# Expert weights prepared ahead of pass 0, their low halves on VectorE, and the order of loads and stores in a fused attention and mixture-of-experts kernel

## The chip, the cores and the metric

One core of a Trainium2 chip runs the whole program in one launch. The metric is device time in microseconds; shorter is better.

## The reference

Three stages, all in float32, one feeding the next:

```python
# 1. chunked attention: 4 batches x 8 heads x 768 positions x 64;
#    32 queries see 8 memory keys and the keys from 16 before to 8 behind their chunk
out[:, :, c0:c1] = softmax(scale * q_c @ k_full.T) @ v_full
x = out.transpose(0, 2, 1, 3).reshape(3072, 512)
# 2. gated feed-forward: w_gate, w_val (512 x 1536), w_out (1536 x 512)
x = (sigmoid(x @ w_gate) * (x @ w_val)) @ w_out
# 3. eight experts: w1 (8 x 512 x 1024), w2 (8 x 1024 x 512)
P = exp(x @ w_gate2 - max)
for _ in range(8):                 # Sinkhorn over experts and tokens
    P /= P.sum(1, keepdims=True) + 1e-9
    P /= P.sum(0, keepdims=True) + 1e-9
    P *= 3072 / 8
out = sum(P[:, e:e+1] * (relu(x @ w1[e]) @ w2[e]) for e in range(8))
```

## The kernel before

Every large product is made as three matmuls on operands split into a high half `h` (rounded by ScalarE) and a low half `l` (the source less `h`): `operand` (L116) is this pair of instructions, and the engine passed to it makes the low half. Many 2 x 2 block products go by a seven-product scheme, for which `combine` (L120) makes sums of blocks.

The tokens are eight chunks of 384. Chunks 0 and 1 go through feed-forward plainly, then three blocks `b` = 1 to 3 of two chunks each; beside each block runs the attention of later chunks. `hook` (L375) is called 60 times in a block (a tick), and `schedule` lays side work on tick numbers. `paced` (L426) puts what a step issues behind the last gated operand of feed-forward on the same engine. The order of instructions on each engine and of DMA issues on SP (all DMAs are issued there) comes from a planner that runs a timeline simulation while the program is built; `issue_after` adds an order between two instructions of one engine to what it may choose.

The expert stage runs three passes `s` of 1024 tokens over 8 experts with 2 halves `hf` of the hidden layer. A layer (one `e`, `hf`) has two units `fp`. `layer1` (L901) makes a unit's seven products `p` from W1; `layer2` (L970) makes eight token tiles `py` in pass 0, where W2 is used in full, and `layer2_turned` is for passes 1 and 2. The first three products of the next layer's first unit stand ahead of each `layer2`. In pass 0 the weights arrive raw. `ask` (L840) loads a unit's four raw tiles, two units before their use. `w1_operands` (L135) makes seven W1 tiles in the `ws` slots (nine) and stores them to `w1k`; `w2_get` (L862) makes W2's full tiles and stores them to `w2k`; `w2_sums` (L848), a layer2 later, makes the sums for passes 1 and 2 and stores them. For these units GpSimd makes all low halves. Passes 1 and 2 load `w1k` and `w2k` back (`w1_load`, L154; `w2_get`).

The first four units (`EN`, L49) are prepared during blocks 2 and 3 by `early_weights` (L611), ten steps a unit from tick 16 of block 2 on, two ticks apart. It reads each unit's raw W1 and raw W2 twice, 512 KB at a time, and pass 0 loads the results back. `first_x` (L664) makes the operands of three of the seven token sums of pass 0 at ticks 40 to 52 of block 3; `rest_of_x` (L670) makes the others at its end. Both call `x_part` (L176), which fetches a quarter of the tokens with 8 DMAs of 64 KB into one of the two `r` slots and uses it at once.

Sinkhorn (L751) runs beside layers 0 and 1 in 17 steps. `beat` (L797) is called at each of a unit's seven products and at each token tile of layer2; every third call makes a step. Its column sums go through TensorE (`pc`, L775), so TensorE waits there for VectorE's `cs` (L772). The last two steps store the gates for passes 1 and 2.

Of the kernel before, what the change touches and what calls it, by code (L numbers as in the profile page):

```python
# [47 lines left out]
XA, XB = 40, 4  # L48
EA, EB, EN = 16, 2, 4  # L49
XALL = True  # L50
XQ = ()
# [11 lines left out]
def moe_chain(ctx: ExitStack, tc: tile.TileContext, qkv, mask, mrow, mone, wa, wg, wb, out):  # L63
# [70 lines left out]

    def w1_operands(nm, r, pool, kept=None, ce=None, ge=None):  # L135
# [12 lines left out]
        operand(t[6][:, 0], t[6][:, 1], ge, a22)  # L148
        if kept is not None:
            for i in range(TH):  # L150
                nc.sync.dma_start(out=kept[i], in_=flat(t[i]).bitcast(F32))
        return w1_sets(t)

    def w1_load(nm, pool, kept):  # L154
        t = w1_tiles(nm, pool)
        for i in range(TH):
            nc.sync.dma_start(out=flat(t[i]).bitcast(F32), in_=kept[i])
        return w1_sets(t)

    early = {}  # L160
# [15 lines left out]
    def x_part(s, xop, kk, o, which=range(7)):  # L176
        xr = rw.tile([128, 2, 2, XW], F32, tag="r", name=f"xs{s}_{kk}_{o}_{which[0]}")
# [18 lines left out]
    with ExitStack() as c1:  # L196
# [414 lines left out]
        def early_weights(u):  # L611
            nm = "_".join(map(str, u))

# [5 lines left out]
            def split(q, src, n, kept):  # L619
                h = rw.tile([128, 1024], F32R, tag="r", name=f"eh{q}_{nm}")[:, 0:n]  # L620
                l = rw.tile([128, 1024], F32R, tag="st", name=f"el{q}_{nm}", bufs=SB_)[:, 0:n]
                operand(h, l, nc.vector, src)
# [4 lines left out]
            k1, k2 = w1k[u], w2k[u]  # L627
            ve = nc.vector
# [13 lines left out]
            operand(h[:, 0:512], h[:, 512:], ve, ld[:, 0])  # L642
            nc.sync.dma_start(out=k1[0], in_=h[:, 0:512].bitcast(F32))
            nc.sync.dma_start(out=k1[1], in_=h[:, 512:].bitcast(F32))
            h = rw.tile([128, 1024], F32R, tag="r", name=f"ea_{nm}")[:, 0:512]
            operand(h[:, 0:256], h[:, 256:], ve, q[3])
            nc.sync.dma_start(out=k1[6], in_=h.bitcast(F32))
            yield
# [10 lines left out]
            ld, _ = raw(1)  # L659
            yield  # L660
            split("d", flat(ld), 1024, [(k2[0], k2[1], 0, 1024)])
            yield

        def first_x():  # L664
            early["x"] = x_tiles(0, XE)
            for kk, o in parts:
                x_part(0, early["x"], kk, o, XE)
                yield

        def rest_of_x():  # L670
            rest = tuple(i for i in range(7) if i not in XE)
            early["x"].update(x_tiles(0, rest))
            for kk, o in parts:
                x_part(0, early["x"], kk, o, rest)
                yield

        pend = []
        for b in range(1, NCH // 2):
            if b == 2:
                schedule(clock[0] + EA, [paced(early_weights(u)) for u in early_units], EB * 10, range(0, 10 * EB, EB))  # L680
            if b < NCH // 2 - 1:
                schedule(clock[0] + CB[0], [attention(c, hp) for c in (2 * b + 2, 2 * b + 3) for hp in range(4)], CB[1], O3)
            else:
                c3.close()
                early["xe"] = ctx.enter_context(tc.tile_pool(name="xe", bufs=1, side="right", reuse_waits="tile"))
                schedule(clock[0] + XA, [paced(first_x())], XB, range(0, 4 * XB, XB))
# [48 lines left out]
            second(*pend.pop(0), halves=(1,))  # L735
            second(*pend.pop(0))
# [7 lines left out]
    with ExitStack() as c2:  # L744
# [52 lines left out]
        def beat():  # L797
            beats[0] += 1
            if beats[0] % 3 == 1:
# [4 lines left out]
        def x_operands(s):  # L804
            xop = x_tiles(s, range(7))
            for kk in range(2):
                for o in range(0, 512, XW):
                    x_part(s, xop, kk, o)
# [13 lines left out]
        def raw_pair(nm, src):  # L822
            rs = []
            for f, k in enumerate(("sh", "sl")):
                rs.append(s_tile(k, f"{nm}_{f}", F32))
                nc.sync.dma_start(out=rs[f], in_=src[:, f, :])
# [21 lines left out]
        def w2_sums():  # L848
# [9 lines left out]
            operand(th, tl, nc.gpsimd, v.rearrange("p i d -> p (i d)"))  # L858
# [3 lines left out]
        def w2_get(s, e, hf, fp):  # L862
# [11 lines left out]
            nc.sync.dma_start(out=dh.bitcast(F32), in_=kept[0])  # L874
            nc.sync.dma_start(out=dl.bitcast(F32), in_=kept[1])
# [25 lines left out]
        def layer1(s, e, hf, xop, gs, w2):  # L901
# [154 lines left out]
        xop = early["x"]  # L1056
        work = [(s, e, hf) for s in range(NSB) for e in range(E) for hf in range(2)]
# [89 lines left out]
```

## Time and profile before

| | us |
|---|---|
| median of 3 runs (2708.99 to 2713.59) | 2712.32 |
| the profiled execution | 2718.7 |
| its span, first to last instruction | 2716.9 |
| TensorE busy | 2646.9 |
| VectorE busy | 2058.4 |
| ScalarE busy | 1128.1 |
| GpSimd busy | 711.1 |

Feed-forward and attention fill the span to about 790 us, pass 0 of the experts goes on to about 1450 us, pass 1 to about 2070 us, pass 2 to the end. TensorE's busy time is high in every part, so the profile is read by stretches: where TensorE sits idle, what its granted clock is there, and what ended each wait. Busy shares of the other engines only matter where TensorE waits for one of them.

### The profile page before, as it was taken

How to read it: one execution, taken by the hardware profiler on the slowest of the kernel's cores; microseconds unless marked ns; L12 is line 12 of the kernel's file. 1: busy time of each engine (PE TensorE's matmuls, PEld its weight loads, DVE VectorE, ACT ScalarE, POOL GpSimd, SP SyncE). 2: the span in 40 equal slices, each digit the busy share in tenths (PEclk: the TensorE clock that was granted, in tenths of full speed). 3: DMA queues.
4: the chain of work that ended last, by engine and by line, in shares of the span. 5: the costliest groups of instructions: out<-in, count | busy, mean ns of one | idle time of the engine just before them, and what ended most of it. 6: DMA issues, size and time to landing. Idle time of an engine off the chain costs nothing.

```text
span 2716.9 us, 38051 instructions
## 1 busy us (share of the span) xinstructions
PE 2646.9 (97%) x12917; PEld 2238.4 (82%) x12917; DVE 2058.4 (76%) x3479; ACT 1128.1 (42%) x2508; POOL 711.1 (26%) x520
## 2 busy tenths in 40 slices
PE   8999999999988999999999999999999999999999
PEld 6898888999976888888887888888877778888887
DVE  7888788676675666666667788777878777887777
ACT  6666766665342334334334332323233332323232
POOL 0002431000002445445441223222221322222222
PEclk9999999999999999999999999999999999999999
DMA  6446677788864567667667556655666565566544
GB/s 212 156 166 204 229 245 250 241 308 298 298 232 155 197 242 264 228 244 262 229 225 256 189 203 227 233 187 191 231 229 231 207 228 185 194 233 228 208 175 183
DMA packets 272366, 604.80 MB, mean 223 GB/s; under 512 B 29961, under 2 KB 51145, under 8 KB 272172
## 3 DMA queue, kind: packets, MB, share of 16 engines
q1 hardware_dynamic: 272172, 602.37, 62.8%
q8 instruction: 102, 1.67, 0.3%
q14 instruction: 92, 0.75, 0.1%
HBM read 425.99 MB, written 176.26 MB: 222 GB/s over the span
## 4 chain that ended last, share of the span: by engine, by line
PE 81%; DMA 9%; DVE 7%; ACT 2%; issue 1%; SPq 0%; POOL 0%; DVEq 0%; ACTq 0%; POOLq 0%
PE p L925 10%; PE p L926 10%; PE p L927 10%; PE pz L1024 4%; PE py L80 4%; PE py L81 4%; PE py L82 4%; PE pz L1025 4%; PE pz L1026 4%; DMA w2b<-w2k 3%; PE pzr L1026 3%; PE pzr L1024 3%; PE pzr L1025 3%; PE px L81 2%; PE px L82 2%; PE px L80 2%
## 5 line engine op out<-in xcount | busy, mean ns | idle before, releaser
L925 PE MATMUL p<-xh,w 128*128 128x512 f32 x1344 | 520.1, 391 | 6.9 <-ACT ce L947 4.1
L926 PE MATMUL p<-xl,w 128*128 128x512 f32 x1344 | 524.4, 390 | 0.0
L927 PE MATMUL p<-xh,w 128*128 128x512 f32 x1344 | 519.5, 390 | 0.0
L925 PEld LDWEIGHTS p<-xh,w 128*128 128x128 f32 x1344 | 253.0, 188 | 61.9 <-ACT ce L947 4.7
L926 PEld LDWEIGHTS p<-xl,w 128*128 128x128 f32 x1344 | 253.0, 188 | 53.1 <-DVE xl L118 0.8
L927 PEld LDWEIGHTS p<-xh,w 128*128 128x128 f32 x1344 | 252.8, 188 | 53.1 <-DMA w<-w1k 0.3
L1032 DVE TENSOR_TENSOR acc<-pz,acc 128x512 f32<-128x512 f32 x248 | 169.9, 688 | 85.9 <-PE pz L1026 83.0
L80 PE MATMUL py<-w2a,gh 128*128 128x512 f32 x512 | 201.2, 393 | 0.1
L81 PE MATMUL py<-w2b,gh 128*128 128x512 f32 x512 | 200.2, 391 | 0.0
L82 PE MATMUL py<-w2a,gl 128*128 128x512 f32 x512 | 197.7, 391 | 0.0
L118 POOL TENSOR_TENSOR gl<-ce,gh 128x512 fp32r<-128x512 f32 x64 | 94.8, 1481 | 387.9 <-ACT gh L117 387.9
L1032 DVE TENSOR_TENSOR acc<-pzr,acc 128x512 f32<-128x512 f32 x248 | 165.0, 687 | 39.8 <-PE pzr L1026 38.5
L118 POOL TENSOR_TENSOR w2b<-r,w2a 128x512 fp32r<-128x512 f32 x56 | 80.6, 1460 | 421.6 <-PE py L81 409.0
L118 POOL TENSOR_TENSOR sl<-cb,sh 128x512 fp32r<-128x512 f32 x64 | 84.2, 1315 | 306.0 <-ACT sh L117 166.7
L947 ACT COPY ce<-p 128x512 f32<-128x512 f32 x96 | 56.4, 587 | 231.3 <-PE p L927 221.3
L118 POOL TENSOR_TENSOR sl<-cd,sh 128x512 fp32r<-128x512 f32 x64 | 89.0, 1390 | 192.1 <-PE p L926 47.7
L987 DVE SCALAR_TENSOR_TENSOR acc<-py,logit,acc 128x512 f32<-128x512 f32 x112 | 80.2, 744 | 77.7 <-PE py L82 77.0
L118 POOL TENSOR_TENSOR w2d<-wv,w2c 128x1024 fp32r<-128x1024 f32 x28 | 67.5, 2410 | 237.6 <-ACT w2c L117 237.6
L941 ACT COPY cb<-p 128x512 f32<-128x512 f32 x96 | 56.0, 584 | 155.7 <-PE p L927 154.3
L930 DVE TENSOR_TENSOR cd<-p,ce 128x512 f32<-128x512 f32 x96 | 66.1, 689 | 66.4 <-ACT ce L947 62.1
L80 PEld LDWEIGHTS py<-w2a,gh 128*128 128x128 f32 x512 | 97.0, 189 | 20.7 <-DVE acc L987 0.5
L117 ACT CAST sh<-ca 128x512 fp32r<-128x512 f32 x64 | 39.8, 622 | 178.2 <-DVE ca L121 161.5
(301 smaller groups left out, 6931.9 us busy)
## 6 DMA issues: line engine op xcount, KB each, us to landing
w<-w1k SPq DMA_DIRECT2D x476, 256.0 KB
w1k<-w SPq DMA_DIRECT2D x196, 256.0 KB
w2a<-w2k SPq DMA_DIRECT2D x68, 512.0 KB
w2b<-w2k SPq DMA_DIRECT2D x68, 512.0 KB
w2c<-w2k SPq DMA_DIRECT2D x64, 512.0 KB
w2d<-w2k SPq DMA_DIRECT2D x64, 512.0 KB
r<-in_wb SPq DMA_DIRECT2D x112, 256.0 KB
w_g<-wak SPq DMA_DIRECT2D x84, 256.0 KB
```

The lines of the kernel that those rows point to most:

```text
L80: nc.tensor.matmul(ps, wh, xh, start=first, stop=False)
L81: nc.tensor.matmul(ps, wh, xl, start=False, stop=False)
L82: nc.tensor.matmul(ps, wl, xh, start=False, stop=last)
L118: return eng.tensor_tensor(out=l, in0=src, in1=h.bitcast(F32), op=ALU.subtract)
L925: nc.tensor.matmul(ps, wh[:, ks], xh, start=kk == 0 and not more, stop=False, skip_group_check=True)
L926: nc.tensor.matmul(ps, wh[:, ks], xl, start=False, stop=False, skip_group_check=True)
L927: nc.tensor.matmul(ps, wl[:, ks], xh, start=False, stop=kk == 1, skip_group_check=True)
L987: nc.vector.scalar_tensor_tensor(out=dst, in0=src, scalar=pe, in1=dst, op0=ALU.mult, op1=ALU.add)
L1024: nc.tensor.matmul(ps, wh[:, ds], gh, start=fp == 0 and not more, stop=False, skip_group_check=True)
L1025: nc.tensor.matmul(ps, wh[:, ds], gl, start=False, stop=False, skip_group_check=True)
L1026: nc.tensor.matmul(ps, wl[:, ds], gh, start=False, stop=fp == 1, skip_group_check=True)
L1032: nc.vector.tensor_tensor(out=a[q], in0=ps, in1=a[q], op=ALU.add)
```

## The change

Three units are prepared early, by one job that also makes the first token operands: 13 steps from tick 10 of block 2 and 11 from tick 6 of block 3, three ticks apart. Each raw tile is read once and serves both the sums and the plain halves. A token quarter is fetched by `x_raw` one step ahead, in two or three DMAs; the first two quarters for `rest_of_x` are fetched at the end of the job. A Sinkhorn step is made at each second beat. The table for Exp is loaded before the last output product of feed-forward. In pass 0 the low halves of raw units are VectorE's. The stores to `w1k` stand behind the last raw load asked for, and the loads of W2 for early units behind the last load of W1. The first `ask` stands before layer 0, and the next ones from the last early unit on, so the distance stays two units.

```diff
-XA, XB = 40, 4
-EA, EB, EN = 16, 2, 4
+EA, EB, EK, EN = (10, 6), 3, (13, 11), 3
+BT = 2
 def w1_operands(...):
-            for i in range(TH):
-                nc.sync.dma_start(out=kept[i], in_=flat(t[i]).bitcast(F32))
+            with tc.issue_after(last_raw[0].ins) if last_raw[0] else nullcontext():
+                for i in range(TH):
+                    nc.sync.dma_start(out=kept[i], in_=flat(t[i]).bitcast(F32))
-    def x_part(s, xop, kk, o, which=range(7)):
...
-        for kh in range(2):
-            for tb in range(2):
-                for q in range(0, XW, 128):
-                    c, w = divmod(s * SB + tb * 512 + o + q, CT)
-                    nc.sync.dma_start(out=xr[:, kh, tb, q:q + 128], in_=x2d[c][:, 2 * kh + kk, w:w + 128])
+    def x_raw(s, kk, o, nm=""):
...
+        for tb in range(2):
+            q = 0
+            while q < XW:
+                c, w = divmod(s * SB + tb * 512 + o + q, CT)
+                n = min(XW - q, CT - w)
+                nc.sync.dma_start(out=xr[:, :, tb, q:q + n], in_=x2d[c][:, kk::2, w:w + n])
+                q += n
+        return xr
 def early_weights(u):
-            ld, q = raw(0)
-            yield
-            h = rw.tile([128, 1024], F32R, tag="st", name=f"ef_{nm}", bufs=SB_)
...
-            yield
+            split("f", ld[:, 0], 512, [(k1[0], k1[1], 0, 512)], True)
+            split("a", a22, 256, [(k1[6][:, 0:256], k1[6][:, 256:], 0, 256)], True)
             ld, (b11, b12, b21, b22) = raw(1)
...
-            ld, _ = raw(1)
-            yield
             split("d", flat(ld), 1024, [(k2[0], k2[1], 0, 1024)])
-            yield
-
-        def first_x():
+
+        def ahead_of_experts():
+            for u in early_units:
+                yield from early_weights(u)
             early["x"] = x_tiles(0, XE)
-            for kk, o in parts:
-                x_part(0, early["x"], kk, o, XE)
+            xs = [x_raw(0, *parts[0], "f")]
+            yield
+            for n, (kk, o) in enumerate(parts):
+                if n + 1 < len(parts):
+                    xs.append(x_raw(0, *parts[n + 1], "f"))
+                x_part(0, early["x"], kk, o, xs[n], XE)
                 yield
+            early["rest"] = [x_raw(0, *p, "r") for p in parts[:2]]
+            yield
...
+            if b == NCH // 2 - 1:
+                tc.keep_in_program_order(nc.scalar.preload_act_table_set("natural_log_exp_and_others"))
             second(*pend.pop(0))
 def beat():
-            if beats[0] % 3 == 1:
+            if beats[0] % BT == 1:
 def w2_sums():
-            operand(th, tl, nc.gpsimd, v.rearrange("p i d -> p (i d)"))
+            operand(th, tl, nc.vector, v.rearrange("p i d -> p (i d)"))
 def w2_get(s, e, hf, fp):
-                    operand(dh[:, f * 512:(f + 1) * 512], dl[:, f * 512:(f + 1) * 512], nc.gpsimd, r)
+                    operand(dh[:, f * 512:(f + 1) * 512], dl[:, f * 512:(f + 1) * 512], nc.vector, r)
...
-            nc.sync.dma_start(out=dh.bitcast(F32), in_=kept[0])
-            nc.sync.dma_start(out=dl.bitcast(F32), in_=kept[1])
+            with tc.issue_after(last_load[0].ins) if s == 0 else nullcontext():
+                nc.sync.dma_start(out=dh.bitcast(F32), in_=kept[0])
+                nc.sync.dma_start(out=dl.bitcast(F32), in_=kept[1])
 def layer1(...):
-                if s == 0 and units.index((e, hf, fp)) >= EN - 2:
+                if s == 0 and units.index((e, hf, fp)) >= EN - 1:
                     ask()
                 if (e, hf, fp) in raws:
-                    w = w1_operands(nm, raws[e, hf, fp][0], ws, w1k[e, hf, fp], nc.vector)
+                    w = w1_operands(nm, raws[e, hf, fp][0], ws, w1k[e, hf, fp], nc.vector, nc.vector)
...
         xop = early["x"]
+        ask()
```

## Rows read from the trace of the kernel before

**Rows 1.** Section 1 of the page: busy time, share and count by engine.

```profile
PE 2646.9 (97%) x12917; PEld 2238.4 (82%) x12917; DVE 2058.4 (76%) x3479; ACT 1128.1 (42%) x2508; POOL 711.1 (26%) x520
```

**Rows 2.** Windows view: length, busy PE, PEld, DVE, ACT, POOL, granted clock, DMA share, GB/s.

```profile
600.00:650.00 50.00, 47.45 (x278) 43.98 (x277) 40.96 (x85) 29.32 (x72) 0.00 (x0) 0.93 0.82 285
...
700.00:750.00 50.00, 45.97 (x260) 45.16 (x259) 29.98 (x62) 18.22 (x40) 0.00 (x0) 0.99 0.86 289
750.00:800.00 50.00, 43.52 (x217) 37.94 (x216) 37.84 (x94) 20.65 (x48) 0.00 (x0) 0.94 0.69 234
800.00:850.00 50.00, 46.99 (x198) 37.94 (x197) 26.70 (x70) 16.95 (x30) 2.94 (x3) 0.93 0.42 136
850.00:900.00 50.00, 42.09 (x183) 34.62 (x182) 32.16 (x65) 12.45 (x23) 13.29 (x11) 0.93 0.44 148
...
1000.00:1050.00 50.00, 50.00 (x223) 41.40 (x222) 34.74 (x51) 19.48 (x34) 24.32 (x17) 1.00 0.73 260
...
1600.00:1650.00 50.00, 50.00 (x222) 41.39 (x221) 43.22 (x63) 16.32 (x29) 15.29 (x12) 1.00 0.69 259
...
900.00:1400.00 500.00, 500.00 (x2208) 414.16 (x2207) 333.78 (x494) 200.72 (x350) 252.10 (x173) 1.00 0.69 247
```

**Rows 3.** Waits of TensorE from 500 to 910: total us, times, longest.

```profile
PE pc L775 <- DVE cs L772: 9.2, 2, 6.6
PE px L80 <- ACT gh L117: 5.0, 3, 2.6
PE p L925 <- ACT ce L947: 3.8, 2, 2.5
PE p_g L552 <- ACT cgb L570: 2.4, 1, 2.4
```

**Rows 4.** Timeline of SP, 725 to 910: start, us of merged issues, line, transfer, count.

```profile
766.97 9.46 SPq L182 DMA_DIRECT2D xs<-x2d  x17
...
803.01 11.29 SPq L157 DMA_DIRECT2D w<-w1k  x13
...
847.34 0.32 SPq L870 DMA_DIRECT2D w2k<-w2a  x1
...
864.01 1.82 SPq L826 DMA_DIRECT2D r<-in_wb  x4
```

**Rows 5.** Waits of SP's queue from 720 to 910.

```profile
SPq L870 <- ACT w2a L117: 29.4, 2, 28.2
SPq L792 <- ACT gt L790: 25.4, 2, 23.9
```

**Rows 6.** Timeline of VectorE, 800 to 905; in brackets the idle before and its end.

```profile
819.92 0.42 DVE L121 TENSOR_TENSOR wq<-r 128x256 f32<-128x256 f32 x1 [4.00 <-DMA r<-in_wb]
...
869.95 0.42 DVE L121 TENSOR_TENSOR wq<-r 128x256 f32<-128x256 f32 x1 [2.51 <-DMA r<-in_wb]
```

**Rows 7.** GpSimd's groups, 900 to 1400: count, busy us, mean ns, idle before, releasers.

```profile
L118 POOL TENSOR_TENSOR w2b<-r,w2a 128x512 fp32r<-128x512 f32 x50 | 72.7, 1474 | 10.0 <-ACT w2a L117 7.8 <-DMA r<-in_wb 2.2
L118 POOL TENSOR_TENSOR w<-wq,w 128x512 fp32r<-128x512 f32 x48 | 65.6, 1379 | 43.2 <-ACT w L117 32.6 <-DMA r<-in_wb 10.5
L118 POOL TENSOR_TENSOR w2d<-wv,w2c 128x1024 fp32r<-128x1024 f32 x26 | 62.7, 2411 | 202.7 <-ACT w2c L117 202.7
L118 POOL TENSOR_TENSOR w<-r,w 128x512 fp32r<-128x512 f32 x25 | 37.4, 1496 | 21.5 <-ACT w L117 19.1 <-DVE gl L895 2.4
```

**Rows 8.** VectorE's groups in the same stretch.

```profile
L895 DVE SCALAR_TENSOR_TENSOR gl<-cb,gh 128x512 fp32r<-128x512 f32 x25 | 40.4, 1618 | 3.3 <-ACT gh L894 2.6
L121 DVE TENSOR_TENSOR wq<-r 128x256 f32<-128x256 f32 x25 | 30.7, 1226 | 11.0 <-DMA r<-in_wb 11.0
...
L121 DVE TENSOR_TENSOR wq<-wq,r 128x256 f32<-128x256 f32 x24 | 13.9, 578 | 43.0 <-DMA r<-in_wb 43.0
```

**Rows 9.** Early low halves on VectorE, by tile: ns min, median, max, first and last start.

```profile
L118 DVE TENSOR_TENSOR ef<-er,ef x4: 684/689/694, 522.9 to 690.0; 128x512 fp32r<-128x512 f32 x4
...
L118 DVE TENSOR_TENSOR eld<-er,ehd x4: 1218/1220/1221, 552.4 to 714.0; 128x1024 fp32r<-128x1024 f32 x4
```

More of the change, by code (lines that the diff above doesn't have):

```diff
@@ L133, in flat @@
         return t.rearrange("p a b -> p (a b)")
+    last_raw = [None]
     def w1_operands(nm, r, pool, kept=None, ce=None, ge=None):
@@ L156, in w1_load @@
         for i in range(TH):
-            nc.sync.dma_start(out=flat(t[i]).bitcast(F32), in_=kept[i])
+            last_load[0] = nc.sync.dma_start(out=flat(t[i]).bitcast(F32), in_=kept[i])
         return w1_sets(t)
-    early = {}
+    early, last_load = {}, [None]
     early_units = units[:EN]
@@ L174, in x_tiles, with x_part @@
         return t
-    def x_part(s, xop, kk, o, which=range(7)):
-        xr = rw.tile([128, 2, 2, XW], F32, tag="r", name=f"xs{s}_{kk}_{o}_{which[0]}")
-        for kh in range(2):
-            for tb in range(2):
-                for q in range(0, XW, 128):
-                    c, w = divmod(s * SB + tb * 512 + o + q, CT)
-                    nc.sync.dma_start(out=xr[:, kh, tb, q:q + 128], in_=x2d[c][:, 2 * kh + kk, w:w + 128])
+    def x_raw(s, kk, o, nm=""):
+        xr = rw.tile([128, 2, 2, XW], F32, tag="r", name=f"xs{s}_{kk}_{o}{nm}")
+        for tb in range(2):
[6 more added lines that the diff above has]
+        return xr
+    def x_part(s, xop, kk, o, xr, which=range(7)):
         b11, b12, b21, b22 = (xr[:, kh, tb, :] for kh in range(2) for tb in range(2))
@@ L612, in early_weights @@
             nm = "_".join(map(str, u))
+            k1, k2 = w1k[u], w2k[u]
+            ve = nc.vector
             def raw(i):
@@ L617, in raw, with split @@
                 return ld, [ld[:, r, o:o + 256] for r in range(2) for o in (0, 256)]
[L619 to L622, printed above, removed]
+            def split(q, src, n, kept, one=False):
+                l = rw.tile([128, 1024], F32R, tag="st", name=f"el{q}_{nm}", bufs=SB_)
+                if one:
+                    h, l = l[:, 0:n], l[:, 512:512 + n]
+                elif q == "d":
+                    h = rw.tile([128, 1024], F32R, tag="st", name=f"eh{q}_{nm}", bufs=SB_)
+                else:
+                    h = rw.tile([128, 1024], F32R, tag="r", name=f"eh{q}_{nm}")
+                operand(h, l, ve, src)
                 for a, b, o, m in kept:
@@ L658, in early_weights @@
             yield
-            ld, _ = raw(1)
-            yield
-            split("d", flat(ld), 1024, [(k2[0], k2[1], 0, 1024)])
-            yield
-        def first_x():
-            early["x"] = x_tiles(0, XE)
-            for kk, o in parts:
-                x_part(0, early["x"], kk, o, XE)
-                yield
+            split("d", flat(ld), 1024, [(k2[0], k2[1], 0, 1024)])
+        def ahead_of_experts():
+            for u in early_units:
+                yield from early_weights(u)
+            early["x"] = x_tiles(0, XE)
+            xs = [x_raw(0, *parts[0], "f")]
+            yield
+            for n, (kk, o) in enumerate(parts):
[4 more added lines that the diff above has]
+            early["rest"] = [x_raw(0, *p, "r") for p in parts[:2]]
+            yield
         def rest_of_x():
@@ L672, in rest_of_x @@
             early["x"].update(x_tiles(0, rest))
-            for kk, o in parts:
-                x_part(0, early["x"], kk, o, rest)
+            xs = early["rest"]
+            for n, (kk, o) in enumerate(parts):
+                x_part(0, early["x"], kk, o, xs[n], rest)
+                if n + 2 < len(parts):
+                    xs.append(x_raw(0, *parts[n + 2], "r"))
                 yield
@@ L679, in moe_chain @@
             if b == 2:
-                schedule(clock[0] + EA, [paced(early_weights(u)) for u in early_units], EB * 10, range(0, 10 * EB, EB))
+                job = paced(ahead_of_experts())
+            if b >= 2:
+                schedule(clock[0] + EA[b - 2], [job], 0, range(0, EB * EK[b - 2], EB))
             if b < NCH // 2 - 1:
@@ L685, in moe_chain @@
                 early["xe"] = ctx.enter_context(tc.tile_pool(name="xe", bufs=1, side="right", reuse_waits="tile"))
-                schedule(clock[0] + XA, [paced(first_x())], XB, range(0, 4 * XB, XB))
             x = block_operands(b)
@@ L825, in raw_pair @@
                 rs.append(s_tile(k, f"{nm}_{f}", F32))
-                nc.sync.dma_start(out=rs[f], in_=src[:, f, :])
+                last_raw[0] = nc.sync.dma_start(out=rs[f], in_=src[:, f, :])
             return rs
```

10 lines of the change are left out of this document (1 added, 9 removed).

## The prediction

> **What bounds the kernel now.** I began with the busy times: TensorE is busy 2646.9 us of the 2716.9 us span [rows 1]. So the change can gain only where TensorE idles or runs at a reduced clock, and can lose wherever it makes TensorE wait. The next view was busy time by stretches of 50 us, since a mean over the run hides stages. In the stretch from 1000 us, inside pass 0 of the experts, TensorE is busy all 50 us at granted clock 1.00, and all of 900 to 1400 us is busy 500.00 of 500 [rows 2]: nothing can be gained there, however much VectorE or GpSimd does. The losses that this change can reach lie from 600 to 900 us, the end of feed-forward and the first expert layers. I count a stretch's idle plus 50 us times the missing clock share: from 600 us 2.55 + 3.5 = 6.1; from 700 us 4.03 + 0.5 = 4.5; from 750 us 6.48 + 3.0 = 9.5; from 800 us 3.01 + 3.5 = 6.5; from 850 us 7.91 + 3.5 = 11.4 [rows 2]. That is 38 us, the ceiling of the gain in these stretches.
>
> Then I asked whom TensorE waited for there. The largest entry is the Sinkhorn matmul `pc` waiting for VectorE's `cs`, 9.2 us in two waits, the longer 6.6; after it come feed-forward waits for ACT's `gh` (5.0) and `cgb` (2.4), and 3.8 on `ce` in the experts [rows 3]. Such a wait names the last engine only. VectorE's own order of time shows what held `cs`: before each of the two stalls VectorE sat at `wq`, the first sum on a raw weight, until a raw load landed (4.00 and 2.51 us idle) [rows 6]. SP's queue shows why the loads are late: 17 token loads take 9.46 us of issuing from 767 us, then thirteen `w1k` loads 11.29 us from 803 us [rows 4]. The first store of unit 4's W2 holds SP for 28.2 us until 847 us, waiting for ACT; raw loads for the next unit follow at 864 us [rows 4, 5].
>
> **The change part by part.**
>
> *Startup of the experts (800 to 900 us, 17.9 us lost).* Sinkhorn has 17 steps. One step each third beat puts the last two `pc` at beats 37 and 40; one each second beat puts them at 25 and 27. Beats are the 7 products of a unit and the 8 token tiles of a layer: layer 0 is beats 1 to 14, then 3 products ahead, layer2 of layer 0 is 18 to 25. So the last `pc` moves from the start of the second layer2 to just behind the first, before the load at 864 us that held it. I take back 8 of the 11.4 us of that stretch: the 6.6 us wait and some of its clock. The first of the two stalls is less sure, since unit 4 is still asked for at unit 2, but the queue ahead is shorter: unit 3's seven `w1k` and two W2 loads become four raw ones, asked for before layer 0, the W2 loads stand behind the W1 loads, and token loads are fewer. I take 3.5 of 6.5 us. Unit 3's stores (3.75 MB) join the pass later; as SP's waits for 28.2 us and for the gates' 23.9 us [rows 5] left TensorE fully busy soon after, I cost them at nothing. Their cover is the spare of the `ws` slots; without it the price is one wait like that on `ce`, 2.5 us at most of the 3.8.
>
> *End of feed-forward (700 to 800 us, 14.0 us lost).* Each token quarter was fetched by 8 DMAs of 64 KB in the step that used it; now by two or three larger ones, a step ahead. For the first 1024 tokens, which are read twice, 64 issues become 20. At 9.46/17 = 0.56 us an issue [rows 4] SP gets back 44 x 0.56 = 25 us. Operand work on ACT no longer queues behind a load just issued, as the waits for `gh` and `cgb` suggest [rows 3]. The first quarters' work ends at tick 33 of the last block's 60 instead of starting at 40. I take 6 of the 14.0 us; the rest is the handover itself (last products, evictions, logits), which the edit leaves. Two new covers: two raw quarters hold both `r` slots from tick 36, and no other work of that block asks for one; the early job's VectorE steps wait for stores made from the staging slot three ticks before, and were that too short, each would cost about a mean `gh` wait, 5.0 us over three [rows 3]. The Exp table load is put ahead of the last output products: under 1 us either way, inside the rounding.
>
> *Middle of feed-forward (600 to 650 us, 6.1 us lost).* Three early units instead of four, each reading 1 MB raw instead of 2, and none at the block boundary (ticks 46 to 66 are free). I take 1.5 us; bounds 0 and 6.
>
> *Pass changes near 1450 and 2070 us.* 32 token issues become 10 at each. I take 1 us together; bounds 0 and 3.
>
> *Low halves of pass 0 on VectorE.* In 900 to 1400 us GpSimd does about 50 + 48 + 25 of 512 columns and 26 of 1024 [rows 7], and 24 of 256 whose row I leave out. On VectorE a low half of 512 took 0.689 us and one of 1024 1.220 [rows 9]: 123 x 0.689 + 26 x 1.220 = 116 us, and with the small ones, bounded by 0 and 24 x 0.689, some 126. VectorE gets something back: `gl<-cb` takes 1.618 us where GpSimd works beside it [rows 8], against 0.689, and `wq<-r` 1.226 against 0.578 for its sister row: 25 x 0.929 + 25 x 0.648 = 39 us. So VectorE goes from 333.8 [rows 2] to about 421 us of 500, 84%. In the stretch from 1600 us it is busy 43.22 of 50 (86%) and TensorE still 50.00 [rows 2]. On that nearest row the cost is 0; the far end is the second rival below. I take 2 us over the pass. The Trainium skill speaks against this move (Perfetto Trace Analysis, section Optimizing Scalar/DVE Operations): with a saturated VectorE, offloading, even to GpSimd, can be right, though as the two share a port it "might not help". The first half of that would make the second rival come true; the row from 1600 us is against it.
>
> Sum: 8 + 3.5 + 6 + 1.5 + 1 - 2 = 18 us. The profiled execution took 2718.7 us, so 2700.7 for one like it. It lies 6.4 us above the median of 2712.3; less that, **2694 us**.
>
> **The rivals.**
>
> *Stalls form again.* The list of waits names what came last; with `cs` and tokens early, the next late thing is the W2 of unit 1, now queued behind the last W1 load, or raw unit 4. Then startup gives back 5 rather than 11.5 and feed-forward 2 rather than 7.5, so with pass 2 us and 1 us the net is 6: 2706 us, and with one more stall like that of `pc` (6.6) no change: 2712. For it: SP's long waits are an order that the planner chose [rows 5], and it plans again. That the edit's order does not survive the planning falls here too.
>
> *VectorE becomes the bound of pass 0: slower.* Its queue is in order. Low halves that wait for ACT's high half held up only GpSimd: 32.6 + 19.1 + 7.8 = 59.5 us in the 500 [rows 7]. On VectorE they stand in front of evictions from PSUM, and waits for raw loads, 11.0 + 43.0 us [rows 8], stay. VectorE has 500 - 421 = 79 us free; 59.5 + 54.0 = 113.5 do not fit, 34.5 short. Over the pass from 900 to 1460 us that is 39 us: 2694 + 39 = 2733. It decides once 24 us of the 39 remain, that is with some three fifths of those waits not overlapped. Against it: the raw loads now precede the stores, which shortens the 54 us; a planner places a low half behind its high half's end; TensorE rides out waits of up to 4 us today.
>
> *All of it works.* Nearly the whole 38 us and the pass changes: 2694 - 18 = 2676.
>
> **How the numbers follow.** Forecast case (2684 to 2704) 0.52; all of it 0.10; stalls form again 0.22 (half faster, half within 0.2%); VectorE bound 0.16 (2709 to 2733, mostly slower). A measurement of this kernel can tell about 0.2%, 5.4 us, from no change. Faster: 0.52 + 0.10 + 0.11 = 0.73; same: 0.11 + 0.01 = 0.12; slower 0.15. The range goes from 2674, the full gain, to 2720, the first part of the VectorE rival.
>
> **What would show it.** Right: no `pc` wait over 2 us; the 50 us stretches of 700 to 900 us losing some 17 rather than 32 us; token issues on SP 20 before the experts; VectorE 80 to 86% busy in pass 0, GpSimd idle, TensorE 500 of 500; `gl<-cb` near 0.69. Wrong: TensorE losing a few tenths of a microsecond per layer to `ce`, `ca` or `acc` from 900 to 1400 us (the VectorE rival), or new waits of TensorE for `w2a`, `w2b` or `w` before 900 us (stalls form again).

## The result, and the profile after

The median of the changed kernel is 2686.73 us over four runs (2685.41 to 2694.60), against 2711.48 us over four runs of the kernel before (2708.99 to 2713.59): ratio 0.9915, 95% interval 0.9894 to 0.9936; the medians lie 24.8 us apart. The forecast was 2694 us, in a range of 2674 to 2720. The profiled execution of after took 2687.21 us, with a span of 2685.1.

Busy times on the page of after, engine by engine, answering to [rows 1]:

```profile
PE 2631.9 (98%) x12917; PEld 2228.5 (83%) x12917; DVE 2103.9 (78%) x3677; ACT 1136.7 (42%) x2510; POOL 429.8 (16%) x324
```

GpSimd has lost 281 us of work and VectorE has gained 45. TensorE has the same 12917 matmuls. The windows view of after (length, busy PE, PEld, DVE, ACT, POOL, granted clock, DMA share, GB/s), in the stretches of [rows 2]:

```profile
600.00:650.00 50.00, 49.86 (x307) 46.69 (x307) 35.93 (x75) 28.46 (x64) 0.00 (x0) 1.00 0.68 228
...
700.00:750.00 50.00, 49.06 (x278) 47.50 (x276) 34.26 (x78) 20.96 (x47) 0.00 (x0) 1.00 0.70 231
750.00:800.00 50.00, 44.52 (x205) 36.46 (x205) 35.49 (x83) 20.96 (x41) 0.00 (x0) 0.97 0.75 248
800.00:850.00 50.00, 43.55 (x183) 35.03 (x182) 31.16 (x88) 16.30 (x29) 0.00 (x0) 0.93 0.24 91
850.00:900.00 50.00, 50.00 (x223) 41.38 (x222) 38.84 (x73) 18.62 (x32) 0.00 (x0) 1.00 0.70 246
900.00:1400.00 500.00, 500.00 (x2207) 414.03 (x2206) 375.33 (x666) 204.46 (x344) 0.00 (x0) 1.00 0.68 244
```

By the prediction's own measure (idle plus 50 us times the missing clock share), the stretch from 600 us loses 0.1 us where it lost 6.1, from 700 0.9 (4.5), from 750 7.0 (9.5), from 800 10.0 (6.5), from 850 nothing (11.4). That is 38.0 us before and 18.0 after. The stretches from 700 to 900 us lose 17.9, where the prediction asked for some 17. A stretch of time doesn't hold the same work in both kernels, since after runs ahead; the phases below do. From 900 to 1400 us TensorE is busy 500.00 of 500, as before, with VectorE at 75% and GpSimd at zero.

TensorE's waits in after from 500 to 910 us (total us, times, longest), answering to [rows 3]:

```profile
PE pc L791 <- DVE cs L788: 4.8, 2, 3.4
PE px L80 <- ACT gh L117: 4.2, 1, 4.2
PE pg L804 <- DVE logit L796: 1.7, 1, 1.7
PE p L942 <- ACT ce L964: 1.0, 2, 0.6
```

The Sinkhorn wait has halved but is not gone, and three feed-forward waits for `gh` have become one of 4.2 us. VectorE's groups from 900 to 1400 us (count, busy us, mean ns, idle before, releasers), answering to [rows 7, 8]:

```profile
L118 DVE TENSOR_TENSOR w2b<-r,w2a 128x512 fp32r<-128x512 f32 x48 | 31.1, 687 | 13.3 <-DMA w2k<-w2d 13.1 <-ACT w2a L117 0.3
L118 DVE TENSOR_TENSOR w2d<-wv,w2c 128x1024 fp32r<-128x1024 f32 x24 | 29.4, 1225 | 22.4 <-ACT w2c L117 22.3
L912 DVE SCALAR_TENSOR_TENSOR gl<-cb,gh 128x512 fp32r<-128x512 f32 x24 | 16.6, 690 | 1.1
L121 DVE TENSOR_TENSOR wq<-wq,r 128x256 f32<-128x256 f32 x24 | 10.0, 419 | 12.2 <-DMA r<-in_wb 12.2
L121 DVE TENSOR_TENSOR wq<-r 128x256 f32<-128x256 f32 x23 | 9.6, 417 | 0.0
```

The low halves take what the early ones took [rows 9]. Their neighbours have become shorter: `gl<-cb` 1618 to 690 ns, `wq<-r` 1226 to 417, `wq<-wq,r` 578 to 419. The wait for raw weights has gone from 54.0 us [rows 8] to 12.2. Other waits of VectorE have come in with the low halves: 22.3 us for ScalarE's `w2c`, 14.4 for its `w`, and 13.1 until a store has left the slot of `w2b`. They fit into the 125 us that VectorE is idle.

Waits and busy time hide the clock and the small gaps, so I also worked out one loss for each phase. For each matmul it is the time from its start to the next one's, less a short such time for its shape (0.226 us with 512 columns, 0.173 with 384; for every shape the time that a fifth of its matmuls in all profiles stay within), summed over the phase. Up to 680 us the phases are cut by time, from there by the number of the matmul, since times shift between kernels: "layer 0" is the first 180 matmuls `p` and `py` of the experts, "behind" the next 260, up to just behind the second `layer2`. The row "before again" is a second profile of the kernel before (below).

```
us lost        <150  150-430 430-590 590-680 680-experts | layer 0 behind | pass 0 chg 0/1 pass 1 chg 1/2 pass 2 | all
before          50.6   39.9    19.3     9.9      12.8    |  11.1   10.9   |  2.3    3.7     8.0   12.4   12.3 | 193.4
before again    45.5   39.2    18.1     9.1      11.3    |  11.5   10.5   |  2.4    4.1    10.2    9.1   16.2 | 187.2
after           45.2   40.2    15.3     4.5       9.0    |   8.6    5.6   |  1.5    1.8     7.8    9.8   12.0 | 161.5
```

Between "before again" and after, 25.7 us lie between the spans (2710.8 and 2685.1), and the table says where: 7.4 us from 430 to 680 us, 2.3 up to the experts, 7.8 in layer 0 and behind, 3.2 in the rest of pass 0 with the change to pass 1, and 5.9 in passes 1 and 2. The last has to be read with care: the two rows of the same kernel before differ by 3.9 us in pass 2 and 3.3 at the change before it.

### The profile page after: what moved, and what is told of

Read it like the earlier page. It is cut to its first block, busy times and chain, and to the rows that moved or that the text cites. A ratio compares the mean times of both kernels' runs of the same rounds, so it can differ in the third digit from the quotient of the medians.

```text
span 2685.1 us, 37559 instructions
## 1 busy us (share of the span) xinstructions
PE 2631.9 (98%) x12917; PEld 2228.5 (83%) x12917; DVE 2103.9 (78%) x3677; ACT 1136.7 (42%) x2510; POOL 429.8 (16%) x324
## 4 chain that ended last, share of the span: by engine, by line
PE 85%; DVE 6%; DMA 6%; ACT 1%; issue 1%; SPq 0%; POOL 0%; DVEq 0%; ACTq 0%; POOLq 0%
PE p L942 11%; PE p L943 10%; PE p L944 10%; PE pz L1041 4%; PE py L80 4%; PE py L81 4%; PE pz L1042 4%; PE py L82 4%; PE pz L1043 4%; PE pzr L1043 3%; PE pzr L1041 3%; PE pzr L1042 3%; DMA w2b<-w2k 3%; PE px L81 2%; PE px L82 2%; PE px L80 2%
## 5 line engine op out<-in xcount | busy, mean ns | idle before, releaser
L953 ACT COPY ca<-p 128x512 f32<-128x512 f32 x96 | 56.4, 587 | 136.9 <-PE p L944 135.7
L82 PEld LDWEIGHTS py<-w2a,gl 128*128 128x128 f32 x512 | 96.8, 189 | 20.3
L81 PEld LDWEIGHTS py<-w2b,gh 128*128 128x128 f32 x512 | 96.7, 189 | 20.1
```

The lines of the kernel that those rows point to most:

```text
L81: nc.tensor.matmul(ps, wh, xl, start=False, stop=False)
L82: nc.tensor.matmul(ps, wl, xh, start=False, stop=last)
```

## The experiments

**The kernel before again.** No edit.

> The kernel before once more, for a second profile: its profiled execution lay 6 to 7 us above the median, and to 450 us, where both kernels issue the same instructions in the same order, TensorE lost 6.5 us more in it than in the changed one. Theory: that is between executions, so this profile loses less before 450 us and is near 2711 us. Rival: the changed plan itself speeds up the first 450 us, and this profile loses there as the first one did.

Measured: 2712.59 us, span 2710.8. It is the base for what follows, since it starts like after. The first 150 us lose 45.5 us rather than 50.6, with the same instructions (last section). Each kernel below has its own runs of before beside it; their medians go from 2709.40 to 2714.41 us, so two changed kernels are compared by their ratios to before, not by their medians.

**Low halves back on GpSimd, all else as in after.**

```diff
-operand(th, tl, nc.vector, v.rearrange("p i d -> p (i d)"))
+operand(th, tl, nc.gpsimd, v.rearrange("p i d -> p (i d)"))
...
-operand(dh[...], dl[...], nc.vector, r)
+operand(dh[...], dl[...], nc.gpsimd, r)
...
-w = w1_operands(nm, raws[e, hf, fp][0], ws, w1k[e, hf, fp], nc.vector, nc.vector)
+w = w1_operands(nm, raws[e, hf, fp][0], ws, w1k[e, hf, fp], nc.vector)
```

> The changed kernel with the low halves of raw units back on GpSimd in pass 0, all else kept. Theory of the prediction: those halves cost and bring nothing, since TensorE is never idle from 900 to 1400 us in either kernel; 2687 us, within 3 us. Rival, GpSimd was itself a brake (1.4 us for a half, and VectorE held up beside it): startup stalls come back, 2693 us or more, with new waits for w or w2b before 900 us.

Measured: 2693.24 us (2692.28 to 2706.43), ratio to before 0.9929 [0.9913, 0.9946]. Layer 0 loses 11.5 us (after: 8.6), the change to pass 1 3.4 (1.8). The windows view, 900 to 1400 us:

```profile
900.00:1400.00 500.00, 500.00 (x2207) 414.01 (x2207) 319.97 (x489) 201.66 (x343) 259.17 (x172) 1.00 0.67 247
```

Two of VectorE's waits there (total us, times, longest):

```profile
DVE wv L121 <- POOL w L118: 27.5, 11, 3.9
DVE wq L121 <- DMA r<-in_wb: 27.3, 13, 3.1
```

My theory, that the engine of the low halves changes nothing, is neither refuted nor borne out: by the ratios this kernel is 0.14% above after, 3.8 us, and the two intervals overlap. The waits of TensorE for `w` before 900 us that the rival asked for aren't there. Inside pass 0 it does change nothing, TensorE being at 500.00 with GpSimd busy 259.17 us. With GpSimd in the loop VectorE waits 27.5 us for GpSimd's `w` and 27.3 for raw weights, and TensorE rides this out. The losses at both ends of the pass come from the profile of this kernel's longest execution, 13 us above its median, of which the slower start explains 5.6; how much of them is the edit's is not shown.

**Low halves on VectorE alone, in the kernel before.** The same three calls, the other way round.

> The kernel before with one edit alone: the low halves of raw units on VectorE. Theory: VectorE about 84% busy in pass 0 and TensorE still 500 of 500 from 900 to 1400 us; 2711 us, within 3 us. Rival, VectorE becomes the bound once the raw loads come late as they do there: 20 us or more slower, with TensorE idle in each layer. A second rival, the quicker halves help the startup: 3 us or more faster.

Measured: 2709.31 us over ten runs (2703.18 to 2713.99), ratio 0.9985 [0.9974, 0.9996]: about 3 us faster. The windows view, 900 to 1400 us:

```profile
900.00:1400.00 500.00, 500.00 (x2208) 414.01 (x2207) 376.99 (x675) 213.15 (x350) 0.00 (x0) 1.00 0.68 249
```

VectorE's group of the first raw sums there:

```profile
L121 DVE TENSOR_TENSOR wq<-r 128x256 f32<-128x256 f32 x25 | 10.5, 421 | 11.4 <-DMA r<-in_wb 11.4
```

This is the test of the rival that VectorE becomes the bound, and it falls: 376.99 us of VectorE and TensorE still at 500.00, in the old order of loads. The raw wait drops from 54 to 11.4 us by the change of engine alone. The change to pass 1 loses 1.2 us, against 3.7 and 4.1. Layer 0 and the part behind it lose 21.3 us together, against 22.0 in both profiles of before.

**A Sinkhorn step at each third beat, as before.** `BT = 2` becomes `BT = 3`.

> The changed kernel with a Sinkhorn step at each third beat instead of each second. Theory: the last column sums meet the raw load of the next unit again, so the wait of pc for cs comes back near the start of the second layer2; 6 to 8 us slower, 2693 to 2695 us. Rival, the DMA order alone had removed that wait: within 2 us of 2687. A third way: wider steps leave VectorE time between two pc, and it is faster by some 2 us.

Measured: 2691.11 us (2684.61 to 2692.21), ratio 0.9916 [0.9899, 0.9933], against 0.9915 [0.9894, 0.9936] for after. The 6 to 8 us I put on the rate of the steps aren't there. Its longest wait of TensorE from 500 to 910 us:

```profile
PE pc L791 <- DVE cs L788: 8.1, 2, 4.2
```

TensorE's timeline shows where: three pairs of `pc` in a row, with no product between them.

```profile
842.05 0.28 PE L791 MATMUL pc<-cs,ones 128*128 128x8 f32 x2
846.59 0.39 PE L791 MATMUL pc<-cs,ones 128*128 128x8 f32 x2 [4.25 <-DVE cs L788]
850.78 0.60 PE L791 MATMUL pc<-cs,ones 128*128 128x8 f32 x2 [3.81 <-DVE cs L788]
```

The waits for `cs` are larger (8.1 us, after 4.8), but layer 0 loses only 2.7 us (8.6) and the part behind it 12.7 (5.6). The two together are 15.4 against 14.2 us: the rate of the steps moves the loss from the first layer2 to the second, and one microsecond of difference is less than two executions differ by. How much that is, this kernel shows too: up to 798 us every engine and SP's queue have the instructions of after in the order of after, and yet it loses 11.9 us from 680 us to the experts where after loses 9.0.

**A mix of both**: each third beat in layer 0, each second one from there, and the second half of the token work two ticks later.

```diff
-schedule(clock[0], [rest_of_x()], 1, range(4))
+schedule(clock[0] + 2, [rest_of_x()], 1, range(4))
...
-if beats[0] % BT == 1:
+if beats[0] % 3 == 1 if beats[0] < 18 else beats[0] % 2 == 0:
```

> The changed kernel with two shifts: a Sinkhorn step at each third beat in layer 0 and at each second from layer2 of layer 0 on (with each third beat everywhere TensorE lost 2.7 us instead of 8.6 in layer 0, but 12.7 instead of 5.6 behind it), and rest_of_x two ticks later, since its operand work stands among the last gates where px waits 4.2 us for gh. Theory: 3 to 6 us of the first expert layers and 2 us at the end of feed-forward come back; 2679 to 2683. Rival: VectorE is as full wherever the steps stand, so pc waits in another place and the tokens' late operands hold layer 0 instead; within 3 us of 2687, or slower.

Measured: 2693.64 us (2688.54 to 2697.12), ratio 0.9930 [0.9909, 0.9950]. I had hoped for 2679 to 2683. Layer 0 loses 2.7 us again, the part behind it 14.9, and the end of feed-forward 11.1, so neither shift pays. VectorE's order of time in this kernel ahead of the longest stall (start, us, line, operation, tiles, idle before), where a Sinkhorn round is L793 to L796, L783 to L786, then `cs`:

```profile
836.21 0.16 DVE L793 TENSOR_SCALAR cr<-pc 128x8 f32<-128x8 f32 x1
836.28 0.68 DVE L118 TENSOR_TENSOR w2b<-r,w2a 128x512 fp32r<-128x512 f32 x1
836.88 0.68 DVE L118 TENSOR_TENSOR w<-r,w 128x512 fp32r<-128x512 f32 x1
837.49 0.20 DVE L794 RECIPROCAL cr<-cr 128x8 f32<-128x8 f32 x1
837.60 0.64 DVE L912 SCALAR_TENSOR_TENSOR gl<-cb,gh 128x512 fp32r<-128x512 f32 x1
838.15 1.29 DVE L118 TENSOR_TENSOR w2b<-r,w2a 128x512 fp32r<-128x512 f32 x2
839.36 0.17 DVE L795 TENSOR_SCALAR cr<-cr 128x8 f32<-128x8 f32 x1
...
842.72 0.49 DVE L788 TENSOR_REDUCE cs<-logit 128x8 f32<-128x192 f32 x1
```

Nothing here waits for long; the round simply shares VectorE's queue with low halves and raw sums. From `cr` to the end of `cs` it takes 7.0 us (836.21 to 843.21). In after, nearly alone on the queue, such a round took 3.4 us (807.15 to 810.50; VectorE's timeline of after):

```profile
807.15 0.17 DVE L793 TENSOR_SCALAR cr<-pc 128x8 f32<-128x8 f32 x1 [0.48 <-PE pc L791]
...
809.41 0.68 DVE L118 TENSOR_TENSOR w<-wq,w 128x512 fp32r<-128x512 f32 x1
810.01 0.49 DVE L788 TENSOR_REDUCE cs<-logit 128x8 f32<-128x192 f32 x1
```

But 3.4 us is also the whole of after's longest `pc` wait. TensorE's timeline around that round, in after and, for the longest wait, in before:

```profile
806.73 0.39 PE L791 MATMUL pc<-cs,ones 128*128 128x8 f32 x2
810.55 0.39 PE L791 MATMUL pc<-cs,ones 128*128 128x8 f32 x2 [3.43 <-DVE cs L788]
```

```profile
868.40 0.28 PE L775 MATMUL pc<-cs,ones 128*128 128x8 f32 x2
875.25 0.59 PE L775 MATMUL pc<-cs,ones 128*128 128x8 f32 x2 [6.56 <-DVE cs L772]
```

So what is left of the `pc` stalls has two parts. TensorE's order, which the planner makes, puts two rounds side by side with no product between, and TensorE then waits for a whole round, 3.4 us where VectorE is nearly free. VectorE's load while the first raw units are made lengthens the round, here to 7.0 us. A wider spacing of the steps only moves the place; no run changes TensorE's order alone.

**No order between loads and stores.** Both `issue_after` of the change become empty contexts.

> The changed kernel without the two issue_after orders (w1k stores behind the last raw load, W2 loads behind the last W1 load); the planner is free there. Theory: raw loads land later behind stores, W2 loads stand ahead of W1 loads as before; 3 to 4 us slower (2690 to 2691), in 770 to 850 us, and VectorE's wait for raw loads in 900 to 1400 us back toward 54 us with TensorE still 500 of 500. Rival, VectorE is so full that this wait now reaches TensorE: 10 us or more slower, lost in pass 0.

Measured: 2697.53 us (2692.28 to 2701.25), ratio 0.9944 [0.9925, 0.9962]; by the ratios 0.29% above after, 7.9 us, with intervals that overlap by a little. Layer 0 loses 11.7 us rather than 8.6, as the theory asked. Its other half fails: the raw wait of VectorE in pass 0 is 12.6 us and doesn't go back toward 54, so the order is not what shortened it. The rest lies in passes 1 and 2 (18.2 us in pass 2 against 12.0), whose code the edit doesn't touch; their order of instructions differs all the same, since the whole program is planned anew. I can name no mechanism for that part.

**Larger token loads alone, in the kernel before.** The merged loop of `x_raw` put in `x_part`, still at the use.

```diff
-for kh in range(2):
-    for tb in range(2):
-        for q in range(0, XW, 128):
...
+for tb in range(2):
+    q = 0
+    while q < XW:
+        c, w = divmod(s * SB + tb * 512 + o + q, CT)
+        n = min(XW - q, CT - w)
+        nc.sync.dma_start(out=xr[:, :, tb, q:q + n], in_=x2d[c][:, kk::2, w:w + n])
+        q += n
```

> The kernel before with the token quarters fetched in two or three DMAs instead of eight, at the place of use as before. Theory: about half of the feed-forward end's gain of 6 us comes from SP's time and the pass changes give 1 us: 2 to 4 us faster, 2707 to 2709. Rival, fetching ahead is what counts: within 1 us of 2711.

Measured: 2706.22 us over eight runs (2701.70 to 2711.50), ratio 0.9982 [0.9970, 0.9995]: about 4.3 us faster. The end of feed-forward loses 8.3 us (before: 11.3 and 12.8), layer 0 5.3 (11.1 and 11.5). Layer 0 and the part behind it lose 15.5 us together, against 22.0, and all profiles sort by this edit: with the larger loads the two lose 14.2 to 17.7 us, without them 21.3 to 22.5.

**Token loads at their use, in after**: each `x_raw` stands in the call that uses it, none a step ahead.

```diff
-x_part(0, early["x"], kk, o, xs[n], XE)
+x_part(0, early["x"], kk, o, x_raw(0, kk, o, "f"), XE)
-early["rest"] = [x_raw(0, *p, "r") for p in parts[:2]]
```

> The changed kernel with each token quarter fetched in the step that uses it (still in two or three DMAs) instead of one step ahead. Theory: ACT waits again for tokens at the end of feed-forward: 3 us slower, 2690. Rival, the planner had room anyway and merging was enough: within 1 us of 2687.

Measured: 2694.92 us (2692.46 to 2696.23), ratio 0.9931 [0.9915, 0.9948], by the ratios 0.16% above after, 4.3 us, with intervals that overlap. Its profile has the slower first 150 us (50.7), so the phases are set side by side without that one: 430 to 590 us lose 17.4 us (after 15.3), the part behind layer 0 6.9 (5.6), the others are within 1 us. All together this profile loses 2.7 us more than after there. The end of feed-forward, where I had expected the cost, loses 9.1 us, as after does (9.0). So loading ahead is worth 3 to 4 us at most, and by the overlap of the intervals it may be worth nothing.

**No early load of the Exp table.** The two lines of it are removed from after.

> The changed kernel without the early load of the Exp table. Theory: under 1 us, 2687 to 2688; the table load of 1.28 us stands on ACT in the first expert layer, and shows as a wait of TensorE for ce or ca of at most that. Rival, it holds the Sinkhorn chain and with it pc: 2 us or more.

Measured: 2691.02 us (2685.99 to 2696.08), ratio 0.9919 [0.9901, 0.9937]. It can't be told from after.

**Early steps across the block boundary.** In after, the job's steps go to ticks 22 to 58 of block 2 and 2 to 32 of block 3: `EA = (22, 2)` for `(10, 6)`.

> The changed kernel with the early job's steps moved across the boundary of blocks 2 and 3: ticks 22 to 58 and 2 to 32 instead of 10 to 46 and 6 to 36. The gain of the middle of feed-forward was larger than forecast: TensorE loses about 15 and 4.5 us in 430 to 590 and 590 to 680 us, against 18 to 19 and 9 to 10 before. Theory: the free boundary gives it, since the block's operand work fills VectorE there; the loss of 590 to 680 us goes back to 8 us or more, and the time is 4 us longer, 2690 to 2691. Rival, fewer bytes and one unit less give it: the loss stays under 6 us there, 2687.

Measured: 2696.11 us (2694.83 to 2698.06), ratio 0.9940 [0.9917, 0.9963]. From 590 to 680 us it loses 8.3 us, where after loses 4.5 and before 9.1 and 9.9, as the theory of the free boundary asked. The windows view, which shows idle and clock of TensorE back:

```profile
600.00:650.00 50.00, 47.70 (x283) 43.89 (x281) 41.50 (x86) 28.91 (x62) 0.00 (x0) 0.97 0.83 291
```

**Four early units in after**, closer to the boundary: `EK, EN = (15, 15), 4`.

> The changed kernel with four early units instead of three, at the same pace (15 steps in each block, ticks 10 to 52 and 6 to 48, the boundary still free). Theory of the free boundary: 590 to 680 us loses as little as with three units (under 6 us), and the rest is even: one raw unit less in the expert stage against one more before it; 2687, within 3 us. Rival, the number of units counts: 8 us or more lost from 590 to 680 us, 2691 or more.

Measured: 2693.57 us (2687.58 to 2702.28), ratio 0.9923 [0.9900, 0.9946]. From 590 to 680 us it loses 8.9 us, which I had not expected of ticks 10 to 52. ScalarE's timeline shows why:

```profile
608.93 0.62 ACT L117 CAST elf<-er 128x512 fp32r<-128x512 f32 x1 [2.23 <-DVE els L118]
...
615.84 0.41 ACT L117 CAST ela<-er 128x256 fp32r<-128x256 f32 x1 [2.40 <-DMA w1k<-els]
...
617.77 0.51 ACT L117 CAST gh<-cve 128x384 fp32r<-128x384 f32 x1
```

TensorE's timeline in the same stretch:

```profile
618.33 1.51 PE L80 MATMUL px<-gh,hwo 128*128 128x384 f32 x6 [3.51 <-ACT gh L117]
```

The steps ran late and reached the boundary after all. Two casts of an early unit stand in ScalarE's queue there, hold it for 2.23 and 2.40 us, and the `gh` behind them comes 3.51 us late for TensorE.

**Raw tiles read once, in the kernel before.** The body of `early_weights` from after: four units still, seven steps each instead of ten, ticks as before.

> The kernel before with each early unit's raw tiles read once (four units, unit starts 20 ticks apart as before, seven steps each; the third unit's steps still cross the block boundary). Theory of the free boundary: reading once alone leaves the loss of 590 to 680 us at 8 us or more; 2710, within 2 us. Rival, the bytes count: that loss falls under 6 us, and the kernel is 4 us faster, 2707.

Measured: 2706.41 us over ten runs (2700.79 to 2712.19), ratio 0.9973 [0.9959, 0.9987], 8 us below its runs of before. From 590 to 680 us it loses 4.9 us; I had expected 8 or more, as its ticks still cover the boundary. The windows view:

```profile
600.00:650.00 50.00, 49.84 (x305) 45.73 (x304) 40.69 (x87) 31.53 (x71) 0.00 (x0) 1.00 0.80 275
```

VectorE's order of time again, early instructions of this kernel that stand nearest to the boundary:

```profile
594.96 1.21 DVE L118 TENSOR_TENSOR eld<-er,ehd 128x1024 fp32r<-128x1024 f32 x1
...
615.39 0.76 DVE L121 TENSOR_TENSOR eq<-er 128x256 f32<-128x256 f32 x2
```

Between these two neither VectorE nor ScalarE has an early instruction. In after the gap is longer still, to 638.75 us. The profiles sort by this. Kernels with early casts and sums among the operands of the new block (before twice, steps across, four units) lose 8.3 to 9.9 us from 590 to 680 us, and in each TensorE waits for `gh` or `gl` between 611 and 621 us, up to 3.5 us at a time; the rest of the loss is the granted clock, 0.93 to 0.97 from 600 to 650 us where it is 1.00 in the other two. The two without lose 4.5 and 4.9, and TensorE has no wait there at all. The other kernels made from after or before, whose ticks weren't touched, fall in line: 4.4 to 4.5 us and 9.7 to 10.1. It is not the traffic: the kernel with raw tiles read once still moves 275 GB/s from 600 to 650 us and loses little, the one with four early units moves 233 and loses 8.9.

## Why the prediction was right, and where not

The forecast lies 7.3 us above the median. The sign is right, and 20 of the 25.7 us between the profiles lie before pass 1, in the stages it named. Point by point:

**Where gains can lie: right.** TensorE was full from 900 to 1400 us before and after, and the gain came from the ends of stages.

**Startup of the experts, 11.5 us taken back: 7.8 measured, and mostly by another edit.** The step that failed is that moving the last `pc` "from the start of the second layer2 to just behind the first" gives back 8 us. The `pc` did move there, but with the old rate of steps the kernel is as fast within its interval, and the two phases lose 15.4 us instead of 14.2. The prediction also asked for no `pc` wait over 2 us; there is one of 3.4. I had read [rows 6] as "a raw load is late", which is 2.51 of the 6.56 us of the longest wait in before. The raw load is early now, but two rounds still stand side by side in TensorE's order, and VectorE makes raw sums, evictions and low halves between the parts of a round. The other step, 3.5 us from a shorter queue on SP, is the one that was borne out, and too small: the larger token loads alone give back 6 us of layer 0 in the kernel before. The order of loads and stores (3.1 us in layer 0) and the low halves (2.9) stand on one profile each; kernels that leave the startup as it is in after lose 14.2 to 16.0 us in the two phases, those two 17.3 and 17.5. The parts overlap: their sum, 12, is more than the 7.8 that the whole change gained there.

**End of feed-forward, 6 us: right by the stretches, too large by phases.** The stretches from 700 to 800 us lose 7.9 us instead of 14.0, as taken. The phases put 2.3 us up to the first expert matmul, since after reaches it earlier and part of the gain is counted behind. Of the causes forecast, loads ahead of use show nothing here (9.1 us without them, 9.0 with). Fewer issues, 20 on SP for the first 1024 tokens, may be one: merging alone brings the phase to 8.3 us. But the kernel with raw tiles read once and the old token loads comes to 8.3 as well, so which edit gave this gain stays open. What is late next is the 4.2 us wait of TensorE for `gh` at 752 us; VectorE and ScalarE are then full of the token quarters' sums, splits and casts. The handover I had left as it was still costs the rest.

**Middle of feed-forward, 1.5 us with bounds of 0 and 6: mis-sized.** It gave 7.4 us (430 to 680 us), the second largest term. I had named the cause, no early step at the boundary, and given it little; it acts through ScalarE's and VectorE's queues, where early casts stand ahead of `gh`. The stretch from 600 us went from 6.1 us lost to 0.1, the upper bound. The 2.8 us from 430 to 590 us have no experiment of their own.

**Low halves on VectorE, 2 us lost: sign wrong, nothing lost and perhaps a few us gained.** VectorE came to 375 us of 500, not 421. I had let two groups recover (39 us) where all operations with both inputs in SBUF that ran beside GpSimd's recovered: by the numbers above `wq<-r` loses 809 ns rather than the 648 I took, and `wq<-wq,r`, which I had used as the undisturbed row at 578, itself falls to 419. Together these groups gave back some 63 us. Operations that read a product from PSUM had nothing to give back: `acc<-py` takes 743 ns before and 747 after. The rest of the difference is in the sum itself: successive VectorE instructions overlap in the record, so that those of after add up to 416 us where the engine is busy 375 (before: 356 and 334), and mean durations can't be added to a busy time. The Trainium skill (SBUF — State Buffer, section Who interferes with whom) says that VectorE's second port pair is GpSimd's only one and works as an exclusive lock; the rows agree in direction, 1618 to 690 ns for `gl<-cb`. The Trainium skill's other page that I weighed (Perfetto Trace Analysis, section Optimizing Scalar/DVE Operations) says that moving work between the two "might not help"; here it cost nothing, and it helped by about 3 us in the kernel before, while in after its worth, 3.8 us by the ratios, is not clear of noise. The raw waits that I had feared would stay (54 us) fell to 11.4 with the engine alone. In before, SP's queue waits 46.8 us for GpSimd's `w` ahead of the stores to `w1k` from 900 to 1400 us, and the raw loads stand behind them; that this is what made them late is argued, not shown.

**Pass changes, 1 us: about 2** at the change to pass 1 (4.1 to 1.8), where the kernel with low halves alone reaches 1.2 and the one with larger token loads alone 3.9. So it looks like the low halves' rather than the token loads'. The kernel without the early Exp table, with after's low halves, loses 3.8 there too, so this isn't firm. At the second change after isn't better (9.8 against 9.1).

**The rivals.** VectorE as the bound of pass 0 is refuted, by after and by the low halves alone: of the 113.5 us of waits that were not to fit, 12.2 for raw loads and 37 for ScalarE's high halves are left, with 13.1 of a new kind for stores. "Stalls form again" is in part what happened, at `pc` and `gh`: for startup and the end of feed-forward the forecast took 17.5 us, that rival 7, and the phases show 10.1. What kept the sum up is the block boundary. "All of it" (2676) would have needed the 17 us that 750 to 850 us still lose.

**The subtraction of 6.4 us** from the profiled execution to the median was right for a reason I hadn't looked for: that execution lost 5.1 us more in its first 150 us than the second profile of the same kernel.

So the parts up to the change to pass 1 came out near the result because their errors nearly cancel: startup and end of feed-forward too large by 7 us, startup with its larger part on the wrong edit besides, the block boundary too small by 6, the rest of pass 0 with its end too small by 4. The 7 us that the forecast falls short are about what lies in passes 1 and 2, 5.9 us in the pair of profiles, for which it had at most a part of its 1 us. That part stays open. Of the whole change's 0.85%, three of its parts alone in the kernel before bring 0.15% (low halves), 0.18% (larger token loads) and 0.27% (raw tiles read once), 0.60% if they add up, which no run tests. Two profiles of the kernel before differ by 3.9 us in pass 2 alone, and edits that leave that pass's code alone moved it by up to 6.2 us.

## What to carry to other kernels

Side work that a program lays between stages must leave the stage boundary free on every engine's queue that the new stage's operands pass; look for its casts and sums by time on ScalarE and VectorE, not for its bytes. A wait of the matrix engine that names a small reduction was not cured here by issuing that reduction sooner: look first whether the matrix engine has other work between two links of the chain, then count what else stands on the reduction's engine. Before costing a move of two-input work from GpSimd to VectorE, let all operations with both inputs in SBUF that run beside GpSimd recover in the sum, also the one that looks undisturbed, and don't add mean durations to a busy time. Compare two kernels phase by phase only beyond what two executions of the same order differ by, here 3 to 4 us.

## What the runs showed of the hardware

The same instructions start at different speeds. In both kernels every engine has the same instructions up to block 2, and yet the stretch from 50 to 75 us comes in two forms. The windows view of that stretch, in the second profile of the kernel before and in the kernel with token loads at their use:

```profile
50.00:75.00 25.00, 22.88 (x147) 18.97 (x146) 22.36 (x48) 14.18 (x49) 0.00 (x0) 0.93 0.53 185
```

```profile
50.00:75.00 25.00, 22.90 (x118) 19.23 (x117) 18.14 (x38) 10.86 (x37) 0.00 (x0) 0.69 0.48 165
```

TensorE is busy the same 22.9 us, at a granted clock of 0.93 or 0.69, and gets 147 or 118 matmuls done. At 55 us TensorE waits 1.7 us for `gh` in both of them; then the clock stands at its lower level, 1.2 GHz, for 13.7 us in the slower form, as in all profiles that have it, and for 3.4 us in the second profile of before. The first 150 us lose 44.5 to 47.4 us in the one form and 50.6 to 50.9 in the other. Five of the fourteen profiles have the slower start, and in four of them (the first of before, low halves on GpSimd, four units, low halves in before) the profiled run is the longest of its kernel's. Some 5 us of a single run of this kernel, as much as most parts of this change are worth, are decided there. What decides it no run shows.

VectorE's operations with both inputs in SBUF also slowed more beside GpSimd than expected: the sum `wq<-r` of 128x256 went from 417 ns to 760 with GpSimd at work in the new order, and to 1226 in the old, while an eviction with one input in PSUM stayed at 743 to 747.
